# Twelve output stores issued from ScalarE's queue instead of SyncE's, in a windowed-attention and gated-MLP kernel

## The chip, the cores and the metric

The kernel runs on one core of one Trainium2 chip. A core has a matrix engine (TensorE, PE in the profile), three engines for elementwise work (VectorE, DVE; ScalarE, ACT; GpSimd, POOL), an engine that only issues transfers (SyncE, SP) and 16 DMA engines. Each of the five takes its instructions from a list of its own. ScalarE can issue a transfer too: the instruction that does so stands in its list between its arithmetic. An instruction that needs the result of another engine, or the end of a transfer, waits for a semaphore.

The metric is the device time of one execution in microseconds (us), as a median of several runs. Lower is better.

## The reference

Eight batches, eight heads of width 64, 512 local tokens and 32 global tokens for each batch. Global tokens attend to everything, local tokens to the 32 global ones and to the local ones at most 32 places away. The result of attention, 4608 tokens of 512 values, goes through a gated MLP. Cut to what matters:

```
k_all, v_all = concatenate([k_g, k_l]), concatenate([v_g, v_l])
out_g = softmax(q_g @ k_all.T / 8) @ v_all
s_l = concatenate([q_l @ k_g.T / 8, where(|i - j| <= 32, q_l @ k_l.T / 8, -1e9)])
out_l = softmax(s_l) @ v_all
x = concatenate([out_g, out_l]) as 4608 x 512
xn = x / sqrt(mean(x * x) + 1e-6) * rms_g
g, val = xn @ w_gate, xn @ w_val            # 512 -> 1536
out = (g * sigmoid(g) * val) @ w_out        # 1536 -> 512
```

## The kernel before, in words

**Chunks.** The tokens are worked off in nine chunks. Chunks 0 to 7 are the 512 local tokens of one batch each, chunk 8 holds the 256 global tokens of all batches. While the MLP of chunk c is on TensorE, the attention of a later chunk and the norm of chunk c + 1 are woven between its products. In chunks 0 and 1 the weights are also prepared. Weights and activations are split into two fp16 parts each, high and low, and every product is done in three passes (high by high, high by low, low by high).

**The products.** From chunk 2 on, the first layer of a local chunk is done as a 2 x 2 block product by seven products instead of eight (`moe_pair`, results in the banks `pq`). From chunk 3 on the second layer is done by seven products as well (`moe_out`, L1547 to 1640, results in the banks `pr`); chunk 8 has a plain first layer (`moe_f`, results `p`) and this second layer at half the width. Chunks 0 to 2 store their outputs by other code, which is not touched.

**Inside the second layer.** The seven products are numbered. Numbers 1, 5 and 6 are summed alongside each other, and then 2, 7, 3 and 4 are added onto the banks of 1, 6, 5 and 6. As a number ends, `rest(p)` evicts it: 1 gives a tile `os` (ScalarE), 6 gives `oq` (ScalarE, then GpSimd) and the second half of `os` (VectorE). The two output tiles `oo0` and `oo1` hold the two halves of the chunk's tokens: 2 gives one half of `oo0` (ScalarE), 7 one half of `oo1` (VectorE), 3 the other half of `oo0` (VectorE), and then `store(0)` is called, 4 the other half of `oo1` (VectorE), and then `store(1)`. A store of chunks 3 to 7 moves 256 x 512 float32 (512 KB) to the output, one of chunk 8 half of that. That makes twelve stores.

**The next chunk's operands.** Its activations `x` (for chunk 8 `xg`) become fp16: `xh` is the high part, a cast on ScalarE, `xl` the low part, a subtraction of the two on VectorE or GpSimd. The seven-product form also needs sums `h` of blocks, split into `ht` in the same way: a cast on ScalarE, a subtraction on VectorE. In attention, `e` are the exponentials (ScalarE), `sm` their sums, `et` the exponentials transposed (VectorE), and `a` the bank into which TensorE multiplies them by the values `v`.

**What sets the order.** Every call from chunk 1 on is first recorded with its engine by `write` (L1910), under a step's name, and then replayed in the order of hand-written tables, one for each chunk (`_ORDER_1` to `_ORDER_8`). So each engine's list follows the tables, and the profile gives all of these instructions the line of the recorder, L1929. A call that moves to another engine keeps its place in the table and stands in the other engine's list. The loads of weights come from SyncE as well: `fetch` (tiles `wt`, first layer) and `fetch_out` (tiles `wu`, second layer, from the arrays `wa` and `wb`), taken out of a ring when they are due.

**Buffers.** `wt`, `wu`, `os`, `oq`, `oo0`, `oo1` and several tiles of the first layer (`u`, `v`, and others) share one pool of twelve equal buffers (tag `wf`). A new tile takes a buffer whose last users have to be done: for a stored tile that is the end of its transfer.

Of the kernel before, what the change touches and what calls it, by code (L numbers as in the profile page):

```python
# [279 lines left out]
def attention_moe_kernel(  # L280
# [17 lines left out]
    nc = tc.nc  # L298
# [147 lines left out]
    def attn_bank(name):  # L446
        return psum.tile([P, 512], F32, tag="pa", bufs=4, name=name)
# [1099 lines left out]
    def moe_out(ch, c, n, row):  # L1547

        st, w, nj = {}, n // 2, n // 256
        onto = {2: 1, 7: 6, 3: 5, 4: 6}  # L1550

        def bank(p):
            if p not in onto and p not in st:
                if p == 5:
                    st[p] = (
                        attn_bank(f"pr{p}")
                        if c == B
                        else psum.tile([P, 512], F32, tag="pv", bufs=1, name=f"pr{p}")
                    )
                else:  # L1560
                    st[p] = psum.tile([P, 512], F32, tag="po", bufs=2, name=f"pr{p}")
                return st[p], True
            return st[onto.get(p, p)], False

        def products(i):
            for b in (2 * i, 2 * i + 1):
                doing(c, f"O{b}")
                p, g = BLOCKS[b]
                ps, first = bank(p)
                hi, lo = ch["hp"][p, g]  # L1570
                u = ch["wu", b]
                for j in range(nj):
                    for a, x in ((0, hi), (0, lo), (1, hi)):
                        nc.tensor.matmul(
                            ps[:, j * HT : (j + 1) * HT],
                            x[:, j * P : (j + 1) * P],
                            u[:, a, :],
                            start=first,
                            stop=(p in (2, 3, 4) and g == NF // 2 - 1 and a == 1),
                            skip_group_check=True,  # L1580
                        )
                        first = False

        def tile(name):
            t = pool.tile([P, 2, 512], F32, tag="wf", bufs=NF, name=f"{name}_{c}")
            return t

        def part(p):
            return st[onto.get(p, p)][:, : nj * HT]

        def flat(name, i):
            return st[name][:, i, : nj * HT]

        def result(z, h):
            if ("o", z) not in st:
                st["o", z] = tile(f"oo{z}")
            return st["o", z][:, :nj, h * HT : (h + 1) * HT]

        def put(z, h, p, x):
            o = result(z, h)  # L1600
            ps = part(p).rearrange("p (j n) -> p j n", j=nj)
            if x is None:
                nc.scalar.mul(o, ps, inv_k)
            else:
                nc.vector.scalar_tensor_tensor(
                    o, ps, inv_k, x.rearrange("p (j n) -> p j n", j=nj), ALU.mult, ALU.add
                )

        def store(z):
            to = out[row + z * w : row + (z + 1) * w, :].rearrange("(j p) d -> p j d", p=P)  # L1610
            nc.sync.dma_start(to, st["o", z][:, :nj, :])

        def rest(p):
            if p == 1:
                st["s"], st["q"] = tile("os"), tile("oq")
                nc.scalar.mul(flat("s", 0), part(1), inv_k)
            elif p == 6:
                nc.scalar.mul(flat("q", 0), part(6), inv_k)
                nc.vector.scalar_tensor_tensor(
                    flat("s", 1), part(5), inv_k, flat("s", 0), ALU.mult, ALU.add  # L1620
                )
                nc.gpsimd.tensor_tensor(flat("q", 0), flat("q", 0), flat("s", 0), ALU.add)
            elif p == 2:
                put(0, 0, 2, None)
            elif p == 7:
                put(1, 1, 7, flat("s", 1))
            elif p == 3:
                put(0, 1, 3, flat("q", 0))
                store(0)
            elif p == 4:  # L1630
                put(1, 0, 4, flat("s", 0))
                store(1)

        def after(i):
            ended = [p for p, g in BLOCKS[2 * i : 2 * i + 2] if g == NF // 2 - 1]
            if not ended:
                return None
            return lambda: [rest(p) for p in ended]

        return [(lambda i=i: products(i), after(i)) for i in range(len(BLOCKS) // 2)]  # L1640
# [182 lines left out]
    for c in range(NCH):  # L1823
# [3 lines left out]
        for i, un in enumerate(units):  # L1827
# [6 lines left out]
            for name, fn, pe, after in steps:  # L1834
                st = {"name": name, "unit": i, "fn": fn, "pe": pe, "c": c, "x": xi, "after": [], "at": None}
# [83 lines left out]
    def doing(c, step):  # L1919
        if at_work[:2] != [c, step]:  # L1920
            at_work[:] = c, step, 0, ""
# [14 lines left out]
    nc = Written  # L1936
# [231 lines left out]
```

## Time and profile before

| | |
|---|---|
| median of 3 runs | 904.91 us (904.52 to 905.95) |
| profiled execution, its own time | 906.6 us |
| its span, first to last instruction | 904.8 us |
| mean granted TensorE clock in it | 0.991 of full speed |
| TensorE busy | 867.7 us (96%) |
| VectorE busy | 725.8 us (80%) |
| ScalarE busy | 555.3 us (61%) |
| GpSimd busy | 277.2 us (31%) |
| moved by DMA | 212.03 MB, mean 234 GB/s |

How to read the lines that follow in the text: a row of the timeline gives the start of a group of like instructions in us from the start of the span, its length in us, the engine, the line, the operation, the tiles it writes and reads, the shape of one and the count; in brackets stand the idle time of the engine ahead of it and what ended that. Numbers of buffers and chunks are left out of the names, so `oo` is any of the output tiles. `SPq` and `ACTq` are the issues of transfers by SyncE and ScalarE. A row of the waits gives who waited for whom, then the total in us, the count and the longest. The trace puts a wait down to the one that came last.

### The profile page before, as it was taken

What the parts mean: (1) busy time and instruction counts of PE and PEld (TensorE: products, weight loads), DVE (VectorE), ACT (ScalarE), POOL (GpSimd) and SP (SyncE); (2) the same over time, 40 slices, a digit from 0 to 9 for tenths busy, and PEclk for the clock granted to TensorE, in tenths of its full rate; (3) what the DMA queues carried; (4) which work ended last, traced back from release to release, by engine and by line L of the source; (5) the groups of instructions that cost most, each with busy time, mean ns of one, the idle gap of its engine ahead of it and who ended that gap; (6) DMA issues with size and microseconds to landing.
All of it is one profiled execution on the core that took longest, in us unless ns stands there. A gap on an engine that the chain in (4) does not pass through costs nothing. (4 is left out here: it accounts for less than half of the span.)

```text
span 904.8 us, 27760 instructions
## 1 busy us (share of the span) xinstructions
PE 867.7 (96%) x11430; PEld 667.4 (74%) x11430; DVE 725.8 (80%) x1831; ACT 555.3 (61%) x1341; POOL 277.2 (31%) x244
## 2 busy tenths in 40 slices
PE   6699979999999998999999999999999999999998
PEld 4544445545547885588888888888888888888887
DVE  6899998988787687878987888789877886787554
ACT  6899997547354666357665856668565852456232
POOL 0000000033335676515521344223521453134311
PEclk9699999999999999999999999999999999999999
DMA  9983625499277786698778777777876666888675
GB/s 331 406 288 126 196 69 171 153 290 305 75 216 254 224 266 205 195 318 248 222 268 272 247 225 254 267 234 252 282 244 206 227 206 211 261 245 274 218 244 181
DMA packets 101007, 212.03 MB, mean 234 GB/s; under 512 B 8081, under 2 KB 34449, under 8 KB 100881
## 3 DMA queue, kind: packets, MB, share of 16 engines
q1 hardware_dynamic: 100448, 209.94, 70.7%
q8 instruction: 89, 1.46, 0.7%
q10 hardware_dynamic: 432, 0.33, 0.1%
q14 instruction: 38, 0.30, 0.1%
HBM read 183.24 MB, written 27.00 MB: 232 GB/s over the span
## 5 line engine op out<-in xcount | busy, mean ns | idle before, releaser
L1929 PEld LDWEIGHTS <-wt 128*128 128x128 f16 x3312 | 321.6, 98 | 46.3 <-issue 7.0
L1929 PE MATMUL pq<-xh,wt 128*128 128x256 f16 x1152 | 204.0, 273 | 1.3 <-DVE s L1929 1.3
L1929 PE MATMUL pq<-ht,wt 128*128 128x256 f16 x1296 | 156.4, 273 | 1.9 <-DVE v L1929 1.3
L1929 PE MATMUL pq<-xl,wt 128*128 128x256 f16 x576 | 157.0, 273 | 0.0
L1929 ACT ACTIVATE e<-e,sm 128x128 f32<-128x128 f32 x288 | 104.3, 390 | 8.4 <-DVE sm L1929 8.4
L1929 POOL TENSOR_TENSOR e<-e,sm 128x512 f32<-128x512 f32 x24 | 29.2, 1225 | 217.2 <-DVE sm L1929 211.0
L1929 PE MATMUL pr<-wu,hs 128*128 128x256 f16 x792 | 92.6, 273 | 1.2 <-DMA wu<-wb 1.2
L1929 POOL TENSOR_TENSOR hs<-u,hs 128x512 f16<-128x512 f32 x50 | 61.1, 1236 | 97.1 <-ACT hs L1929 92.1
L1929 POOL TENSOR_TENSOR hu<-v,hu 128x256 f16<-128x256 f32 (+1 forms) x60 | 57.1, 966 | 106.3 <-ACT hu L1929 93.0
L1929 PEld LDWEIGHTS <-hs 128*128 128x128 f16 x792 | 77.3, 98 | 10.7 <-issue 1.8
L1929 PE MATMUL pr<-wu,hu 128*128 128x256 f16 x594 | 70.2, 273 | 0.6 <-ACT os L1929 0.6
L1929 ACT ACTIVATE t<-u,half_inv 128x512 f32<-128x512 f32 x72 | 50.3, 718 | 30.9 <-DVE u L1929 29.2
L1929 DVE TENSOR_TENSOR v<-pq,s 128x512 f32<-128x512 f32 x72 | 49.3, 685 | 20.3 <-PE pq L1929 17.4
L1929 PEld LDWEIGHTS <-hu 128*128 128x128 f16 x594 | 57.9, 98 | 7.6 <-issue 0.9
L1929 PE MATMUL po<-wo,h 128*128 128x512 f16 x288 | 63.6, 379 | 0.0
L1651 PE MATMUL p<-xh,wf 128*128 128x512 f16 x192 | 58.8, 379 | 3.4 <-DVE t L1763 1.5
L1929 DVE TENSOR_TENSOR s<-pq,s 128x512 f32<-128x512 f32 x66 | 44.5, 684 | 20.2 <-ACT s L1929 11.2
L1929 ACT COPY s<-pq 128x512 f32<-128x512 f32 x72 | 41.4, 582 | 30.7 <-PE pq L1929 22.2
L1929 DVE SCALAR_TENSOR_TENSOR t<-t,u 128x512 f32<-128x512 f32 x72 | 54.8, 768 | 5.1 <-ACT t L1929 4.9
L1929 PE MATMUL p<-xh,wf 128*128 128x512 f16 x192 | 58.6, 379 | 0.0
L1651 PEld LDWEIGHTS <-wf 128*128 128x128 f16 x288 | 27.7, 98 | 38.2 <-issue 4.4
L1929 ACT COPY u<-pq 128x512 f32<-128x512 f32 x36 | 21.0, 583 | 51.7 <-PE pq L1929 50.9
(380 smaller groups left out, 1704.3 us busy)
## 6 DMA issues: line engine op xcount, KB each, us to landing
wt<-wd SPq DMA_DIRECT2D x120, 512.0 KB, 5.8
wu<-wb SPq DMA_DIRECT2D x36, 512.0 KB, 5.9
wr<-in_w_in_dram SPq DMA_DIRECT2D x24, 512.0 KB, 8.9
wu<-wa SPq DMA_DIRECT2D x24, 512.0 KB, 4.6
k<-in_qkb_dram SPq DMA_DIRECT2D x24, 448.0 KB, 7.1
gkq<-in_gkq_dram SPq DMA_DIRECT2D x16, 576.0 KB, 7.5
wt<-wd SPq DMA_DIRECT2D x36, 256.0 KB, 4.4
v<-in_vb_dram SPq DMA_DIRECT2D x24, 352.0 KB, 5.6
```

What stands on the lines that cost most here:

```text
L1651: nc.tensor.matmul(ps[:, :n], rows[:, a, o : o + P], ch[z][k][:, :n], start=(k == 0 and i == 0), stop=(k == NK - 1 and i == 2),)
L1929: return lambda *a, **k: write(self.engine, lambda: call(*a, **k))
```

## The change

In `store(z)` of `moe_out`, the transfer is issued by ScalarE instead of SyncE. Its place in the order of calls is the same, and so are its source, its target and its size.

```
         def store(z):
             to = out[row + z * w : row + (z + 1) * w, :].rearrange("(j p) d -> p j d", p=P)
-            nc.sync.dma_start(to, st["o", z][:, :nj, :])
+            nc.scalar.dma_start(to, st["o", z][:, :nj, :])
```

SyncE's list loses twelve instructions and ScalarE's gains them; the lists of VectorE, GpSimd and TensorE keep their order. In the rows below a name's numbers are its kind, its chunk or pair, and the buffer; `out_0_dram` is the output.

First, ScalarE's list in the second layer of chunk 4, around the eviction of product 1 (`os_4`) and product 6 (`oq_4`), with the semaphores that each waits for:

```order
@@ -528,6 +530,6 @@
 L1929 CAST hu5_2928<-v_5_2904 128x1024
 L1929 CAST hs5_2930<-u_5_2907 128x1024 [waits DVE_49]
-L1929 ACTIVATE os_4_2939<-pr1_2912,kk_91 128x512 [waits DMAHW0_49,PE_49,DMAHW3_49,Activation_49,Pool_49]
-L1929 ACTIVATE oq_4_2940<-pr6_2924,kk_91 128x512 [waits PE_49,Pool_49]
+L1929 ACTIVATE os_4_2939<-pr1_2912,kk_91 128x512 [waits DMAHW7_49,PE_49]
+L1929 ACTIVATE oq_4_2940<-pr6_2924,kk_91 128x512 [waits PE_49,DMAHW0_49,Activation_49,Pool_49]
 L1929 ACTIVATE e1201_2937,sm12_2914<-e1201_2937,sm12_2914 128x128 [waits DVE_49] x2
```

No instruction moved, but the shared pool hands `os_4` another buffer: it no longer waits for GpSimd (`Pool`), and `oq_4` waits as before for GpSimd and for a transfer besides.

Second, the same list some twenty rows later, at the store of `oo1` of chunk 4, among the exponentials `e1210` and `e1211` of a later chunk's attention:

```order
@@ -526,4 +528,5 @@
 L1929 CAST xh53_2953<-x5_2_2901 128x512
 L1929 ACTIVATE e1210_2931<-e1210_2931,sm12_2914 128x128 x4
+L1929 DMA out_0_dram<-oo1_4_2956 128x2x512
 L1929 ACTIVATE e1211_2945<-e1211_2945,sm12_2914 128x128 x4
 L1929 CAST xh55_2943<-x5_0_2773 128x512
```

The store now stands between the two groups of four, and the second group and the cast `xh55` stand behind it.

Third, ScalarE's list at the end of chunk 6, where `xh7` and `ht7` are operands of chunk 7:

```order
@@ -705,5 +711,7 @@
 L1929 CAST xh72_3314<-x7_2_3277 128x512
 L1929 ACTIVATE oo0_6_3316<-pr1_3288,kk_91 128x2x256
+L1929 DMA out_0_dram<-oo0_6_3316 128x2x512
 L1929 CAST xh73_3318<-x7_2_3277 128x512
+L1929 DMA out_0_dram<-oo1_6_3321 128x2x512
 L1929 CAST ht77_3311<-h7_4_3313 128x512
 L1929 COPY s6_0_3330<-pq6_0_3326 128x512
```

Both stores come in, and the cast `ht77` stands behind the second. At the end of chunk 3 it is alike: the store of `oo1_3` stands ahead of the cast `xh45`. In chunk 5 that of `oo1_5` stands ahead of ScalarE's half of `oo0_5`.

Fourth, ScalarE's list at the end of chunk 7, where `xh8` are operands of chunk 8 and `t` belong to its first layer:

```order
@@ -771,6 +779,8 @@
 L1929 CAST xh81_3476<-xg_77 128x256
 L1929 CAST xh82_3477<-xg_77 128x256
+L1929 DMA out_0_dram<-oo1_7_3483 128x2x512
 L1929 CAST xh83_3478<-xg_77 128x256
 L1929 ACTIVATE oo0_7_3471<-pr1_3449,kk_91 128x2x256
+L1929 DMA out_0_dram<-oo0_7_3471 128x2x512
 L1929 ACTIVATE t1_3493<-p0_1_3491,half_inv_79 128x256
 L1929 ACTIVATE t0_3487<-p0_0_3486,half_inv_79 128x256
```

The store of `oo1` stands ahead of the cast `xh83` and of ScalarE's half of `oo0`. In chunk 8 the two stores are the last instructions of ScalarE's list.

## The prediction

> **What bounds the kernel now.** I read the busy table first, then what TensorE (PE) waits for in the part of the run in which the changed stores stand, then the groups of the stored tiles, then the timeline around each store. The busy table:
>
> ```profile
> span 904.8 us, 27760 instructions
> ...
> PE 867.7 (96%) x11430; PEld 667.4 (74%) x11430; DVE 725.8 (80%) x1831; ACT 555.3 (61%) x1341; POOL 277.2 (31%) x244
> ```
>
> PE is the bound. The matmul waits from 460 us to the end, in which all twelve stores fall, have as columns the total, the count and the longest, in us:
>
> ```profile
> PE pq L1929 <- DVE v L1929: 1.3, 1, 1.3
> PE pq L1929 <- DVE s L1929: 1.3, 1, 1.3
> PE pr L1929 <- DMA wu<-wb: 1.2, 1, 1.2
> PE pr L1929 <- ACT os L1929: 0.6, 1, 0.6
> ```
>
> PE stands still there for 4.4 us in 445, and none of it is put down to a store. So moving stores can win at most a little, and what holds PE up anywhere is paid for in full. The stores themselves, as waits of SyncE (SP) and as a group:
>
> ```profile
> SPq L1929 <- DVE oo L1929: 43.9, 12, 7.5
> ...
> L1929 SPq DMA_DIRECT2D out_dram<-oo x12: 338/378/389, 475.5 to 901.9; - x12
> ```
>
> Each store waits on SP for VectorE's (DVE's) last half of its tile, 43.9 us over twelve, and takes 0.34 to 0.39 us to issue. ScalarE's (ACT's) issue is in the trace too, once beside SP's and once behind another of its own:
>
> ```profile
> 0.73 0.41 ACTq L326 DMA_DIRECT2D mask<-in_masks_dram  x1
> 0.74 0.39 SPq L665 DMA_DIRECT2D q<-in_qk_dram  x1
> 1.17 0.46 ACTq L328 DMA_DIRECT2D gcol<-in_rms_g_dram  x1
> ```
>
> I take 0.41 us for an issue on ACT and 0.04 us per hand-over. The second ACT issue starts 0.03 after the first ends; other hand-overs below show up to 0.08.
>
> **Part by part.** The bytes are the same, and the twelve issues leave SP. On ACT a store brings two prices: its issue, and its wait for DVE, during which ACT, which takes its instructions in their order, starts nothing that stands behind. Whether that reaches PE depends on those instructions. I go through the places in the order of the chunks.
>
> Chunk 3. The second store stands ahead of the cast xh45 that begins the last operands of a first-layer product:
>
> ```profile
> 477.34 0.61 ACT L1929 CAST xh<-x 128x512 f16<-128x512 f32 x1
> ...
> 478.88 0.75 DVE L1929 SCALAR_TENSOR_TENSOR oo<-pr,kk,os 128x512 f32<-128x512 f32 x1 [1.45 <-PE pr L1929]
> ...
> 479.55 0.71 DVE L1929 TENSOR_TENSOR xl<-x,xh 128x512 f16<-128x512 f32 x1
> ...
> 481.41 0.27 PE L1929 MATMUL pq<-xl,wt 128*128 128x256 f16 x1
> ```
>
> The tile is ready at 479.63 (478.88 + 0.75). Then 0.04, 0.41 of issue, 0.04, 0.61 of cast, 0.04, 0.71 of the subtraction and 0.04 give 481.52, against PE's 481.41: **+0.11**. Before, the cast was done ahead of time.
>
> Chunk 4, a gain. The pool of tiles hands os another buffer (the order below the diff shows its waits change), one that GpSimd (POOL) does not read:
>
> ```profile
> 553.30 1.47 PE L1929 MATMUL pr<-wu,hu 128*128 128x256 f16 x12
> ...
> 555.92 0.69 ACT L1929 ACTIVATE os<-pr,kk 128x512 f32<-128x512 f32 x1 [3.68 <-POOL hu L1929]
> ...
> 556.66 2.12 PE L1929 MATMUL pr<-wu,hu 128*128 128x256 f16 x18 [0.57 <-ACT os L1929]
> ```
>
> os then starts when PE has ended its sum, at 554.77, and is done by 555.5, over 1 us before PE wants the bank back: **−0.57**, the gap in brackets.
>
> Chunk 4, the loss. The second store stands between two groups of four exponentials; the later group is wanted by two transposes and then by PE:
>
> ```profile
> 570.05 1.26 ACT L1929 ACTIVATE e<-e,sm 128x128 f32<-128x128 f32 x4
> ...
> 571.37 0.70 DVE L1929 SCALAR_TENSOR_TENSOR oo<-pr,kk,os 128x512 f32<-128x512 f32 x1
> 572.00 1.28 DVE L1929 STREAM_TRANSPOSE et<-e 128x512 f32<-128x512 f32 x2
> ...
> 573.92 0.82 PE L1929 MATMUL a<-et,v 32*64 32x256 f32 x27
> ```
>
> Ready at 572.07; plus 0.04 + 0.41 + 0.04 + 1.26 + 0.04 + 1.28 + 0.04 is 575.18, against 573.92: **+1.26**. DVE takes the transpose of the later group first, so both count.
>
> Chunk 5. The second store stands ahead of ACT's half of the other tile:
>
> ```profile
> 669.75 0.75 DVE L1929 SCALAR_TENSOR_TENSOR oo<-pr,kk,os 128x512 f32<-128x512 f32 x1 [1.25 <-PE pr L1929]
> ...
> 672.14 0.37 ACT L1929 COPY x<-a 128x256 f32<-128x256 f32 x1 [3.29 <-PE a L1929]
> ...
> 675.89 1.47 PE L1929 MATMUL pq<-ht,wt 128*128 128x256 f16 x12
> ```
>
> ACT was idle for 3.29 us up to 672.14, so the issue (from 670.54) and that 0.7 us half (the same form's 0.69 below) end by 671.8, inside the idle time. PE uses the bank at 675.89: **0**. Without that cover it would be about 1.1.
>
> Chunk 6. The second store stands ahead of the cast ht77, and DVE's difference ht and subtraction xl follow that cast in one line:
>
> ```profile
> 763.02 0.62 ACT L1929 CAST ht<-h 128x512 f16<-128x512 f32 x1
> ...
> 766.02 0.74 DVE L1929 SCALAR_TENSOR_TENSOR oo<-pr,kk,os 128x512 f32<-128x512 f32 x1
> 766.68 0.68 DVE L1929 TENSOR_TENSOR ht<-h,ht 128x512 f16<-128x512 f32 x1
> 767.28 0.69 DVE L1929 TENSOR_TENSOR xl<-x,xh 128x512 f16<-128x512 f32 x1
> ...
> 768.48 0.27 PE L1929 MATMUL pq<-xl,wt 128*128 128x256 f16 x1
> ```
>
> Ready at 766.76; plus 0.04 + 0.41 + 0.04 + 0.62 + 0.04 + 1.29 (ht and xl, 766.68 to 767.97) + 0.04 is 769.24, against 768.48: **+0.76**. The cast xh73 stands between the two stores and now runs behind the first one's issue; if that pushes the second by an issue's length, it is 0.41 more.
>
> Chunk 7. The store of oo1 stands ahead of the cast xh83, POOL's subtraction follows that, and PE needs both for chunk 8:
>
> ```profile
> 851.47 0.40 ACT L1929 CAST xh<-xg 128x256 f16<-128x256 f32 x1 [2.13 <-DVE xg L1929]
> 851.95 0.67 POOL L1929 TENSOR_TENSOR xl<-xg,xh 128x256 f16<-128x256 f32 x1 [0.80 <-ACT xh L1929]
> 852.22 0.69 ACT L1929 ACTIVATE oo<-pr,kk 128x512 f32<-128x512 f32 x1 [0.35 <-PE pr L1929]
> ...
> 856.15 0.75 DVE L1929 SCALAR_TENSOR_TENSOR oo<-pr,kk,os 128x512 f32<-128x512 f32 x1 [4.38 <-PE pr L1929]
> ...
> 857.04 0.27 PE L1929 MATMUL p<-xl,wt 128*128 128x256 f16 x1
> ```
>
> Here the wait is longest: ACT cast at 851.47, and now stands still until 856.90. Then 0.04 + 0.41 + 0.04 + 0.40 + 0.08 (ACT's end at 851.87 to POOL's start) + 0.67 + 0.04 give 858.58, against 857.04: **+1.54**.
>
> The two last stores. DVE's last half is the end of the work:
>
> ```profile
> 901.35 0.48 DVE L1929 SCALAR_TENSOR_TENSOR oo<-pr,kk,os 128x256 f32<-128x256 f32 x1 [1.43 <-PE pr L1929]
> ```
>
> The last store leaves at 901.83 either way: 0.41 on ACT for at most 0.39 on SP, **0** (to within 0.1).
>
> SP gets its 43.9 us of waits back, so loads that stood behind stores go earlier. Only the 1.2 us wait for wu could gain: between nothing, as I take it, since that load waits for its buffer (rivals), and −1.2.
>
> The sum is 0.11 − 0.57 + 1.26 + 0.76 + 1.54 = **+3.10 us**, on the profiled run: span 904.8 to 907.9. That run lies 1.8 us above its span and 1.7 above the median of 904.91; the same addition there gives **908.0 us**. Hand-overs of 0 or of 0.08 in place of 0.04 move the four places by 0.5 each way, and chunk 6 can add 0.4: the forecast's own range is 907.4 to 909.0.
>
> The Trainium skill, page "DMA: Bandwidth & Descriptors", section "Issuing engines are not separate DMA queues", says that DMAs started from several engines run on the same DMA engines and that this saves only the sequencer's time to initiate. By that rule twelve issues of 0.378 us, 4.5 us of SP, are all that changes, and the kernel stays at 904.9. It doesn't count the wait that the sequencer takes along, which by the SP row is ten times as large.
>
> **Rivals.** *No change (0.15).* PE had gaps of its own after two of the places, 1.3 and 1.3 us at pq and 1.2 at wu, and a stall before a gap can come out of it. The wait for wu traces back to PE itself in the chain of waits:
>
> ```profile
> 732.87 0.59 ACT u L1929
> ...
> 746.27 2.11 POOL hu L1929 x2
> 748.38 6.85 DMA wu<-wb
> ```
>
> ACT's u here follows PE's own product, then POOL, then the load, so a PE that is late makes this wait late too; that speaks against. If instead the 1.3 and the 1.2 swallow chunk 4's term and ACT's casts are partly ahead, 906.2 to 906.7 is left. The Trainium skill's rule above, taken alone, would put it here at 904.9.
>
> *Faster (0.04).* If ACT did not hold later instructions while a store waits, the losses vanish, and os' 0.57 and the 1.2 of wu are won: 904.91 − 1.8 = 903.1, just at the bound of what counts as faster below. Against it: the wu load starts at 748.38, behind POOL and not behind a store, and ACT's idle brackets show it waiting in line.
>
> *Slower still (0.09).* An issue of SP next to DMA traffic can take far longer than 0.4:
>
> ```profile
> 767.26 2.25 SPq L1929 DMA_DIRECT2D wt<-wd  x1
> ```
>
> In chunks 3, 4 and 6 SP's next load now starts together with the store on ACT, as both wait for the same end on DVE. If one such issue on ACT is stretched like this (2.25 − 0.41 = 1.8), it gives 909.8; all of the four places, up to 915. Against it: at 0.73 and 0.74 both engines issued at once in 0.41 and 0.39. The point from which it decides is an ACT issue of over 1 us. The Trainium skill's "Perfetto Trace Analysis", section "DMA Instruction — HWDGE (DVE, Sync)", draws such a wait for a shared descriptor block; only the stretched SP row is in keeping with it.
>
> **How the numbers follow.** The forecast has 0.72. About 0.2%, 1.8 us, is what a measurement of this kernel can tell from no change, so the bounds are 903.1 and 906.7. Faster 0.04 and no change 0.15 are the rivals' own chances; the forecast (907.4 and up) and the worse case are slower: 0.81. The range reaches from 906.3, which takes in most of the no-change case that the stalls leave, to 909.8, one stretched issue.
>
> **What would show it.** In the changed trace: PE gaps of about 1.3 before a<-et,v at 574, 0.8 before pq<-xl at 769 and 1.5 before p<-xh or p<-xl at 857, put down to ACT, DVE or POOL; ACT standing still behind DVE oo, 5 us of it in chunk 7; no gap for os near 556; no waits on DVE oo left on SP. I am wrong if PE has no new gaps there, if ACT's store issue is long, or if the gap at 755 goes with the stores.

## The result, and the profile after

| | before | after |
|---|---|---|
| median of four executions each, same comparison | 905.23 us (904.52 to 905.95) | 913.38 us (911.04 to 913.60) |
| ratio, 95% interval | 1 | 1.0073 (1.0056 to 1.0090) |
| profiled execution, its own time | 906.6 us | 913.29 us |
| its span | 904.8 us | 911.2 us |
| mean granted TensorE clock in it | 0.991 | 0.987 |

The kernel is slower, by more than twice the 3.1 us forecast: 0.73% of 905 us is 6.6 us, between 5.1 and 8.1 by the interval. (The ratio is not the quotient of the two medians, which lie 8.15 us apart; this text goes by the ratio.) The side was right, the size and the range were not.

The first lines of the page of after: the same instructions, 6.4 us more span, and TensorE longer at work, which with the same matmuls means a slower clock in places.

```profile
span 911.2 us, 27760 instructions
...
PE 871.4 (96%) x11430; PEld 667.7 (73%) x11430; DVE 727.9 (80%) x1831; ACT 555.6 (61%) x1341; POOL 277.4 (30%) x244
```

What TensorE waited for from 384 us on in after (who, for whom, total, count, longest):

```profile
PE pq L1929 <- DVE xl L1929: 2.0, 1, 2.0
PE pq L1929 <- DVE v L1929: 1.3, 1, 1.3
PE pq L1929 <- DVE s L1929: 1.3, 1, 1.3
PE pr L1929 <- DMA wu<-wa: 0.8, 2, 0.5
PE p L1929 <- ACT xh L1929: 0.7, 1, 0.7
PE a L1929 <- DVE et L1929: 0.7, 1, 0.7
PE p L1929 <- POOL xl L1929: 0.5, 1, 0.5
```

The waits for v and s are those of before. New are the one for xl (chunk 6), for et (chunk 4), and for xh and xl ahead of p (chunk 7): the three places of the prediction. The wait for os is gone. The waits for loads have changed places; more on them below. What ScalarE waited for, and the stores as a group:

```profile
ACT xh L1929 <- DVE oo L1929: 14.7, 3, 8.0
...
L1929 ACTq DMA_DIRECT2D out_dram<-oo x12: 351/378/436, 475.8 to 908.2; - x12
...
DMA to landing us min/median/max: 2.0/5.8/7.0
```

The casts xh waited 14.7 us in three places for a stored tile that they do not read: that is the hold in the queue. The issues themselves are short, 0.35 to 0.44 us, and none is stretched.

**Where the time went, place by place.** I took the start of the same matmul in two traces and the change of the difference from one side of a place to the other (480 to 486 us of before for chunk 3, 554 to 560 for os, 572 to 576 for chunk 4, 758 to 769 for chunk 6, 769 to 771 for what follows it, 856 to 860 for chunk 7). This leaves out what differs elsewhere. In us, with three profiles of the changed kernel (the second and third are runs below):

| place | forecast | after | second | third |
|---|---|---|---|---|
| chunk 3 | +0.11 | +0.51 | +0.50 | +0.50 |
| os of chunk 4 | −0.57 | −0.73 | −0.73 | −0.73 |
| chunk 4 | +1.26 | +1.18 | +1.02 | +1.02 |
| chunk 6 | +0.76 | +2.38 | +2.45 | +2.26 |
| behind chunk 6 | – | +1.42 | +1.35 | +1.54 |
| chunk 7 | +1.54 | +1.52 | +1.51 | +1.51 |
| sum | +3.10 | +6.28 | +6.10 | +6.10 |

From 460 us to the end, where all the stores lie, TensorE loses 6.14, 5.43 and 5.52 us against before in the three profiles. So the places hold the change, and the rest, −0.1 to −0.7 us, is what differs elsewhere, the waits for loads among it. The +1.18 of chunk 4 holds a small gap further on in the product a as well: in the four kernels that leave chunk 4's stores and the order as they were, this window differs from before by −0.13 to +0.45 us.

Chunk 6 and what follows it take 3.80 us in each profile, 3.04 more than forecast. Nearly all that was missed lies there. Its rows in after, ScalarE first, then GpSimd, VectorE and TensorE:

```profile
766.80 0.38 ACTq L1929 DMA_DIRECT2D out_dram<-oo  x1
767.22 0.62 ACT L1929 CAST xh<-x 128x512 f16<-128x512 f32 x1 [4.00 <-DVE oo L1929]
767.40 0.38 ACTq L1929 DMA_DIRECT2D out_dram<-oo  x1
767.82 0.62 ACT L1929 CAST ht<-h 128x512 f16<-128x512 f32 x1
...
767.92 1.16 POOL L1929 TENSOR_TENSOR xl<-x,xh 128x512 f16<-128x512 f32 x1 [8.23 <-ACT xh L1929]
769.03 1.60 POOL L1929 TENSOR_TENSOR ht<-h,ht 128x512 f16<-128x512 f32 x1
...
768.48 1.15 DVE L1929 TENSOR_TENSOR ht<-h,ht 128x512 f16<-128x512 f32 x1 [1.10 <-ACT ht L1929]
769.54 1.64 DVE L1929 TENSOR_TENSOR xl<-x,xh 128x512 f16<-128x512 f32 x1
...
771.23 0.27 PE L1929 MATMUL pq<-xl,wt 128*128 128x256 f16 x1 [1.98 <-DVE xl L1929]
```

In before, GpSimd had the same two operations at another time:

```profile
763.20 1.16 POOL L1929 TENSOR_TENSOR xl<-x,xh 128x512 f16<-128x512 f32 x1 [5.39 <-ACT xh L1929]
764.31 1.16 POOL L1929 TENSOR_TENSOR ht<-h,ht 128x512 f16<-128x512 f32 x1
```

The first store holds the cast xh73, and so GpSimd's pair moves from 763 to 768 (all of TensorE's work is 0.6 us later there) and lies beside VectorE's pair. There VectorE takes 1.15 and 1.64 us for what took 0.68 and 0.69, and GpSimd 1.60 for 1.16. The starts and ends read like turns: VectorE's xl starts at 769.54, GpSimd's ht ends at 770.63, and VectorE ends 0.55 after that. The Trainium skill, page "SBUF — State Buffer", section "SBUF: two separate sides", says that VectorE with two SBUF inputs and GpSimd share a pair of ports as an exclusive lock. By that rule the pairs go one after the other, and the trace agrees, with 1.64 = 1.09 of waiting + 0.55.

Behind the gap TensorE is slow for a while. The windows of after, with TensorE's busy time first and the granted clock as the third number from the end:

```profile
769.00:771.00 2.00, 0.25 (x3) 0.08 (x1) 2.00 (x2) 0.58 (x1) 1.63 (x2) 1.00 0.94 329
771.00:773.00 2.00, 1.77 (x10) 1.31 (x10) 0.78 (x2) 0.58 (x1) 0.00 (x0) 0.63 0.90 348
773.00:775.00 2.00, 2.00 (x12) 1.37 (x11) 0.69 (x1) 0.00 (x0) 0.00 (x0) 0.52 0.53 143
775.00:777.00 2.00, 2.00 (x20) 1.79 (x19) 0.08 (x1) 0.00 (x0) 0.00 (x0) 1.00 0.89 290
```

The clock falls to half after the 1.98 us gap and is back at 775: about 3.4 us at half speed. This costs 1.66 us in each of the three profiles: the 1.4 of the table, and some slow matmuls that lie ahead of the table's border at 769. Up to the matmul that waits, chunk 6 costs 2.14 us.

### The profile page after: what moved, and what is told of

Same layout as the page of the kernel before. It is cut to its first block, busy times and chain, and to the rows that moved or that the text cites. A ratio compares the mean times of both kernels' runs of the same rounds, so it can differ in the third digit from the quotient of the medians.

```text
span 911.2 us, 27760 instructions
## 1 busy us (share of the span) xinstructions
PE 871.4 (96%) x11430; PEld 667.7 (73%) x11430; DVE 727.9 (80%) x1831; ACT 555.6 (61%) x1341; POOL 277.4 (30%) x244
## 5 line engine op out<-in xcount | busy, mean ns | idle before, releaser
L1929 PEld LDWEIGHTS <-hs 128*128 128x128 f16 x792 | 77.2, 98 | 10.2 <-issue 1.1
```

What stands on the lines that cost most here:

```text
L1929: return lambda *a, **k: write(self.engine, lambda: call(*a, **k))
```

## The experiments

Theory H is that of the prediction, with chunk 6 read anew: ScalarE holds everything behind a store until VectorE has ended the tile. Theory Q, the rival: the transfers themselves cost, since on a second queue, beside SyncE's loads, they land late (5.8 us median, 3.8 before) and keep loads and buffers waiting. Where a kernel has some stores on ScalarE and the rest on SyncE, its edit is the line

```
-            nc.sync.dma_start(to, st["o", z][:, :nj, :])
+            (nc.scalar if (c, z) in STORES else nc.sync).dma_start(to, st["o", z][:, :nj, :])
```

with the STORES named below. Ratios are to the kernel before in the same comparison, with 29 or 35 executions of it and 12 of each kernel (6 in each of the two unchanged repeats of after).

**The first store of chunk 6 alone**, STORES = (6, 0).

> Only the first store of chunk 6 (oo0) goes to ScalarE, the other eleven stay on SyncE. Theory H (ScalarE holds what stands behind a store): xh73 is cast after the store, so GpSimd's xl and ht start near 767.5 instead of 763 and run beside VectorE's ht and xl, which then take about 1.1 and 1.6 us instead of 0.68 and 0.69; a PE gap of 1.5 to 2 us ahead of pq<-xl, and a stretch at half clock behind it (another 1.5) where the gap is long enough: 2 to 3.5 us over the kernel before. Theory Q (the stores' transfers on a second queue hold up loads): under 0.3 us, since one store of twelve moved, and no gap at pq<-xl.

1.0011 (0.9994 to 1.0028), at most 2.5 us. In the trace chunk 6 costs 2.17 us and no other place more than 0.13. VectorE and GpSimd:

```profile
766.86 1.23 DVE L1929 TENSOR_TENSOR ht<-h,ht 128x512 f16<-128x512 f32 x1 [1.05 <-ACT ht L1929]
768.01 1.64 DVE L1929 TENSOR_TENSOR xl<-x,xh 128x512 f16<-128x512 f32 x1
...
766.39 1.15 POOL L1929 TENSOR_TENSOR xl<-x,xh 128x512 f16<-128x512 f32 x1 [9.77 <-ACT xh L1929]
767.50 1.60 POOL L1929 TENSOR_TENSOR ht<-h,ht 128x512 f16<-128x512 f32 x1
```

The same overlap as in after, from one store, and a gap of 2.01 us. The clock did not fall behind it here: the next matmuls keep their pace. The last section shows why.

**The second store of chunk 6 alone**, STORES = (6, 1).

> Only the second store of chunk 6 (oo1) goes to ScalarE. Theory H: xh73 is cast early as in the kernel before, GpSimd's xl and ht are done before VectorE's, which keep 0.68 and 0.69 us; only the cast ht77 is late: a PE gap of 0.7 to 0.8 us ahead of pq<-xl, full clock behind it, +0.8 us over the kernel before. If the issue on ScalarE itself were the cost, this and the run with the first store alone would cost the same. Theory Q: under 0.3 us.

1.0016 (1.0001 to 1.0032). Chunk 6 costs 0.75 us in the trace: the 0.76 of the prediction, to a hundredth. VectorE and GpSimd:

```profile
769.65 0.69 DVE L1929 TENSOR_TENSOR ht<-h,ht 128x512 f16<-128x512 f32 x1 [1.13 <-ACT ht L1929]
770.26 0.69 DVE L1929 TENSOR_TENSOR xl<-x,xh 128x512 f16<-128x512 f32 x1
...
764.96 1.15 POOL L1929 TENSOR_TENSOR xl<-x,xh 128x512 f16<-128x512 f32 x1 [4.00 <-ACT xh L1929]
766.07 1.15 POOL L1929 TENSOR_TENSOR ht<-h,ht 128x512 f16<-128x512 f32 x1
```

GpSimd is done before VectorE starts, and both have their old durations. So it is the first store, which the prediction passed over, that makes the dear part.

**All stores on ScalarE, moved to the end of each chunk's order** (chunk 7: only the store of oo1 moved, to the last place):

```
 _ORDER_6 (and likewise 3, 4, 5)
-... R59.0 R59.1 n54.1 n55.0 O41.0 R62.0 R62.1 n55.1 n56.0 n53.1 n52.0
+... R59.0 n54.1 n55.0 O41.0 R62.0 n55.1 n56.0 n53.1 n52.0 R59.1 R62.1
```

> All twelve stores on ScalarE, but in chunks 3 to 7 moved to the end of the chunk's order, behind the casts and exponentials that the next chunk waits for. Theory H: no PE gaps near 574, 769 and 857, full clock there; what is left is the eviction os of chunk 4 without its wait (-0.6) and small waits for loads either way: within 1.5 us of the kernel before, 903.5 to 906.5. Theory Q: the transfers are the same as in the changed kernel and land as late, so most of its 8 us stays: 910 to 913.

1.0025 (1.0005 to 1.0044), 2.3 us: much less than the changed kernel, and yet more than the 1.5 us that theory H allowed. The gaps near 574 and 769 are gone. The expected gain at os did not come, as that tile kept its old buffer. Two other gaps are there, in TensorE's waits:

```profile
PE pq L1929 <- DVE u L1929: 1.4, 1, 1.4
...
PE p L1929 <- DVE t L1929: 0.9, 1, 0.9
```

The second is the hold again: two issues stand at 859.45 ahead of chunk 8's first eviction t. The first is theory Q's: VectorE's v waits there for a semaphore of a transfer and starts when a store of chunk 3 has landed, whose buffer v takes:

```profile
491.41 0.69 DVE L1929 TENSOR_TENSOR v<-pq,s 128x512 f32<-128x512 f32 x1 [4.04 <-PE pq L1929]
492.02 0.68 DVE L1929 TENSOR_TENSOR u<-pq,s 128x512 f32<-128x512 f32 x1
```

The bracket names pq, but in before v starts at 486.61, directly behind s, so its product was done long before. That store was issued at 482.23 and landed at 491.29. So a late store can cost through its buffer, but it does so where it is issued late, not in the changed kernel, where no TensorE gap traces to it.

**The wait without the transfer.** All stores on SyncE; in `store` ScalarE copies two columns that span both halves of the tile to a scratch tile first (the order tables get the extra step behind each store's):

```
+            nc.scalar.copy(seen_o, st["o", z][:, 0, HT - 1 : HT + 1])
             nc.sync.dma_start(to, st["o", z][:, :nj, :])
```

> All stores stay on SyncE; at each store's place ScalarE copies two columns of the stored tile (one from each half) to a scratch tile that nobody reads, so that it waits for VectorE as the store would, without any transfer. The outputs are unchanged. Theory H: the same PE gaps as in the changed kernel, near 574, 769 and 857, each shorter or longer by the difference between this copy (0.2 to 0.3 us) and the store's issue: +5 to +7 us. Theory Q: within 0.5 us of the kernel before.

1.0037 (1.0020 to 1.0054). The copies are short, and ScalarE stands still for VectorE ahead of them:

```profile
L1929 ACT COPY seen<-oo x12: 177/193/194, 479.4 to 908.8; 128x2 f32<-128x2 f32 x12
...
DVE oo L1929: 27.1, 8
```

The places cost +0.22 (chunk 3), +0.76, +1.82 and +1.19 (chunks 4, 6, 7), 4.0 together, with the same releasers on TensorE:

```profile
PE pq L1929 <- DVE xl L1929: 1.7, 1, 1.7
...
PE p L1929 <- POOL xl L1929: 0.5, 1, 0.5
PE p L1929 <- ACT xh L1929: 0.4, 1, 0.4
...
PE a L1929 <- DVE et L1929: 0.3, 1, 0.3
```

That is less than the 5 to 7 expected: by about 0.3 us at each of the four places (in chunk 6 counted up to the matmul that waits), and by the fall of the clock, which does not come behind the 1.66 us gap. The 0.3 is the issue itself: in chunk 7 the cast xh starts 0.10 us after the start of the copy, at 862.60, and in after 0.42 after the start of the store, at 861.78. No transfer moved, and most of the price is there. Wait (4.0), issue (4 x 0.3), clock (1.66) and os (−0.73) add up to the 6.1 of the changed kernel, so nothing is left there for theory Q.

**The changed kernel again**, no edit, for more executions.

> The changed kernel once more, in many executions beside the kernel before on one chip, since single executions of the kernel before spread there from 904.4 to 911.2 us. Theory H with the terms measured so far (chunk 4 +1.2, chunk 6 +2.0 to 2.4, chunk 7 +1.2 to 1.5, os of chunk 4 -0.6, 1.5 to 1.7 more in executions whose TensorE clock drops behind the gap of chunk 6): +4 to +6 us over the kernel before. If the first comparison (+8.15 of four executions each) holds, 3 us more are still to be found: theory Q or another place. PE gaps near 574, 769 and 857 as before; waits for loads near 421, 645, 755 and 828 change from profile to profile.

1.0078 (1.0048 to 1.0108); medians 911.66 and 906.83. The places are the column "second" above.

**All but chunk 6**, STORES = all but (6, 0) and (6, 1).

> Ten stores on ScalarE, the two of chunk 6 on SyncE. Theory H: the run above less chunk 6: no gap ahead of pq<-xl near 769, GpSimd's and VectorE's subtractions apart again, no clock drop there; 2 to 4 us faster than all twelve on ScalarE, +1.5 to +3 over the kernel before. Theory Q: 2 of 12 of the changed kernel's cost less, about 1 us.

1.0031 (1.0017 to 1.0046), 2.8 us where the places sum to 2.3. Chunk 6 costs 0.01 us and the clock stays. Two stores of twelve carry more than half of the price.

**Chunk 4 alone**, STORES = (4, 0), (4, 1).

> Only the two stores of chunk 4 on ScalarE. Theory H: a gap ahead of a<-et,v near 574 that moves PE by 1.2 to 1.3 us; os of chunk 4 keeps its GpSimd wait (0.57), since the buffers ahead of it are as before; +1.2 us over the kernel before. Theory Q: 0.2 to 0.7, and no PE gap at a<-et,v.

1.0026 (1.0006 to 1.0047). The place costs 1.05 us, and os keeps its wait, as expected; the time, 2.4 us by the ratio, is above that, but its interval (0.5 to 4.3) takes it in:

```profile
PE a L1929 <- DVE et L1929: 0.7, 1, 0.7
PE pr L1929 <- ACT os L1929: 0.6, 1, 0.6
```

TensorE starts the product with two matmuls on time and then waits 0.7 us; by the end of the product, 576 us, it is 1.05 late.

**Chunk 7 alone**, STORES = (7, 0), (7, 1).

> Only the two stores of chunk 7 on ScalarE. Theory H: two gaps near 857, one ahead of p<-xh and one ahead of p<-xl, 1.2 to 1.5 us together, ScalarE's cast xh held until VectorE's last half of oo1; +1.3 us over the kernel before. Theory Q: 0.2 to 0.7, and no PE gap.

1.0031 (1.0015 to 1.0047). The place costs 1.54 us, the forecast's figure; the time, 2.8 us by the ratio (1.4 to 4.3), takes it in.

**The changed kernel a third time**, as the measure for the next run.

> The changed kernel, as the measure for the next one, which differs from it in the place of one cast. From the terms measured: c3 +0.4, os -0.7, chunk 4 +1.3, chunk 6 +2.1 and 1.5 for the clock behind it, chunk 7 +1.5, together +6.1 us over the kernel before, between 4.5 and 8 by what the first two comparisons gave.

1.0074 (1.0047 to 1.0101); medians 913.83 and 906.74. Column "third" above.

**The changed kernel with one cast moved**: in chunk 6 the first store goes behind the cast xh73.

```
 _ORDER_6
-... R59.0 R59.1 n54.1 n55.0 O41.0 R62.0 R62.1 ...
+... R59.0 n54.1 n55.0 R59.1 O41.0 R62.0 R62.1 ...
```

> All twelve stores on ScalarE, and in chunk 6 the cast xh73 goes ahead of the first store instead of behind it; nothing else moves. If GpSimd's late subtractions beside VectorE's make the second and larger half of chunk 6's price, they now start about 4 us earlier, VectorE's ht and xl fall from 1.15 and 1.64 to 0.69 and 0.69, the gap ahead of pq<-xl falls from 2.0 to 0.6-0.8 us and the clock does not drop behind it: 2.5 to 3 us faster than the run above. If VectorE's long operations have another cause (the stores' transfers), they stay long and nothing is won.

1.0040 (1.0022 to 1.0057): 3.1 us faster than the run above by the two ratios, 4.0 by the medians (909.87 for 913.83). Chunk 6 costs 0.73 us for 2.26, and nothing behind it for 1.54, together 3.07 less. VectorE and GpSimd:

```profile
770.37 0.69 DVE L1929 TENSOR_TENSOR ht<-h,ht 128x512 f16<-128x512 f32 x1 [1.10 <-ACT ht L1929]
770.98 0.68 DVE L1929 TENSOR_TENSOR xl<-x,xh 128x512 f16<-128x512 f32 x1
...
765.70 1.15 POOL L1929 TENSOR_TENSOR xl<-x,xh 128x512 f16<-128x512 f32 x1 [4.01 <-ACT xh L1929]
766.81 1.16 POOL L1929 TENSOR_TENSOR ht<-h,ht 128x512 f16<-128x512 f32 x1
```

Both stores are still on ScalarE, and only GpSimd's work came out from beside VectorE's. With this the cause of chunk 6 is shown: not the issue, not the transfer, but whom the held cast feeds.

**All stores on ScalarE, each directly behind what the next chunk waits for** (`_ORDER_3`: R62.1 behind n53.1; 4: R62.1 behind n55.0; 6: R59.1 and R62.1 at the end; 7: R62.1 behind R59.0).

> All twelve stores on ScalarE, each directly behind the last instruction that the next chunk waits for: chunk 3 behind xh45 and ht47, chunk 4 behind the second group of exponentials, chunk 6 behind ht77, chunk 7 behind xh83 and ScalarE's half of oo0. Theory H: no gaps near 481, 574 and 769, a gap of up to 0.5 us near 858, where the two issues stand ahead of chunk 8's first eviction; os -0.6. Within 1 us of the kernel before. If stores on ScalarE's queue land late and hold buffers (as in the run with the stores at the chunks' ends, where VectorE waited 1.4 us for a stored buffer), a gap near 490 stays and it is 1 to 2 us slower than before.

1.0020 (1.0005 to 1.0035), 1.8 us where 1 was expected. No gap is left near 481 and 769, 0.34 near 862, as expected. The os gap stayed, against the expectation, and there was a 2.2 us gap within the attention product a, ended by "issue"; the other profiles have 0 to 0.5 us at that matmul, with chunk 4's stores on ScalarE or not. What makes it is open.

**Chunks 3 and 5 alone**, STORES = (3, 0), (3, 1), (5, 0), (5, 1).

> Only the four stores of chunks 3 and 5 on ScalarE. Theory H: os of chunk 4 gets the other buffer and its 0.57 us gap near 556 goes; chunk 3's late cast xh45 costs 0.1 to 0.45 near 481 to 484; chunk 5 nothing. -0.6 to +0.2 us: not to be told from the kernel before by the times, only by the trace.

0.9995 (0.9977 to 1.0012): no difference to be told. In the trace os gains 0.73 and chunk 3 costs 0.50, so the other buffer for os comes from the stores of chunk 3. No version tried is shown to be faster than the kernel before.

## Why the prediction was right in its side and wrong in its size

**The mechanism** was right: TensorE is the bound, the stores' bytes do not matter, and a store that waits in ScalarE's list holds what stands behind it. The wait without a transfer gives most of the price by itself.

**Chunk 4 and chunk 7** were right: 1.26 forecast, 1.02 to 1.18 measured (1.02 at the wait itself in all three profiles), and 1.54 forecast, 1.51 measured. Chunk 7 shows every step of that chain: the store at 861.78 for 0.38, then

```profile
862.20 0.41 ACT L1929 CAST xh<-xg 128x256 f16<-128x256 f32 x1 [8.02 <-DVE oo L1929]
...
862.65 0.27 PE L1929 MATMUL p<-xh,wt 128*128 128x256 f16 x1 [0.71 <-ACT xh L1929]
863.40 0.27 PE L1929 MATMUL p<-xl,wt 128*128 128x256 f16 x1 [0.48 <-POOL xl L1929]
```

The hand-overs are 0.04 here too. **os** was right in kind, −0.73 for −0.57: the bracket counts from the end of the last matmul, which is 0.27 us long, while in a run of matmuls the next starts 0.11 after it. So a gap in brackets is 0.16 short of the delay, here as in chunk 6 (1.98 and 2.14). **Chunk 5 and the last stores** cost nothing, as forecast.

**Chunk 6 is the step that failed**: forecast 0.76, with 0.41 more as the worst that the first store could do. That followed only ScalarE's own list: the cast xh73 would be late, and with it the second store. It didn't follow whom xh73 feeds. GpSimd's two subtractions stood on nobody's path in before, so the working left them out; started 4.7 us later (763.20 to 767.92, 0.6 of it the delay of the whole kernel), they lie beside VectorE's, and VectorE is on the path. This brought 1.4 us (2.14 up to the matmul that waits, for 0.76), and behind the gap, now 2 us long instead of 0.6, the clock fell, another 1.66 that the sum did not have at all. Both together are the 3 us that were missed. The fall is in part luck of the execution (see the last section): without it the places sum to 4.5 us, still above the 2.5 to 4.1 of the forecast's own range.

**Chunk 3** was forecast at 0.11 for xl, and at that matmul PE is late by 0.09. Another 0.42 follows at 484 us, in the global attention's product gs. In the run with chunks 3 and 5 alone it waits 0.3 us for a copy x of VectorE and 0.2 for a copy s of ScalarE. VectorE's copy is late for the reason found in chunk 6. The cast behind xh45 is held too, GpSimd's pair starts at 481.54 in after for 478.55 in before, and beside it VectorE's ht takes 1.65 us for 0.68:

```profile
482.65 1.61 POOL L1929 TENSOR_TENSOR xl<-x,xh 128x512 f16<-128x512 f32 x1
...
483.17 1.65 DVE L1929 TENSOR_TENSOR ht<-h,ht 128x512 f16<-128x512 f32 x1
```

So the same step of the working failed here a second time, in small.

**The rivals.** No change did not come: the waits of TensorE behind the places did not swallow the stalls. The wait of 1.2 us for wu in before, which the prediction weighed, is gone at 755 in all three profiles of the changed kernel, and the prediction had named that as a sign of being wrong. But it is no fixed thing: at the same matmul it is 1.47 and 0 us in the two kernels with one store of chunk 6 moved, where nothing ahead of it had changed. Nor does the load leave earlier: it is issued at 748.38 in before and at 750.26 in after, where TensorE is 1.9 us late; only its landing differs. SP's relief does not show there. The stretched issue did not come either, at most 0.44 us on ScalarE. By the rule of the Trainium skill, page "DMA: Bandwidth & Descriptors", section "Issuing engines are not separate DMA queues", only the time to initiate would have moved; the trace does not agree, since the sequencer's wait moved too, and with what followed from it the change cost 6 us.

**What stays open**: the 2.2 us in one profile, and why the same load lands sooner in one execution than in another. The interval of the measured change, 4.3 to 9.8 us over the three comparisons, holds the 6.1 to 6.3 of the places, but cannot confirm them to better than that.

## What to carry to other kernels

A transfer put into the list of an engine that computes brings its wait along: ask not what the issue costs but what stands behind it, and follow each held instruction to everyone that it feeds, engines with time to spare included, since work that may be late can still land beside work that may not. A store belongs behind the last instruction of its list that somebody waits for, or in a list in which nothing else is urgent. A gap of about 2 us has a price beyond its length in those executions in which the clock falls behind it.

## What the runs showed of the hardware

**The clock falls behind gaps of about 2 us, sometimes.** In fourteen profiles, from 340 us on, ten TensorE gaps of 1.9 to 2.2 us occur. Behind six of them the clock is at half for about 3.4 us, 1.7 us of time lost; behind four it is not. Behind gaps of up to 1.75 us it never is, unless a longer one follows. One of the falls, seen from the gap's end to 3.4 us on, in the third profile of the changed kernel, and then the gap and the stretch behind it in the run with the first store of chunk 6 alone, where the clock stays at 1.00:

```profile
768.40:771.80 3.40, 3.40 (x18) 2.44 (x18) 1.24 (x2) 0.59 (x1) 0.00 (x0) 0.56 0.74 224
771.80:775.00 3.20, 3.20 (x30) 2.76 (x28) 0.69 (x1) 0.00 (x0) 0.00 (x0) 0.93 0.79 282
...
765.60:769.00 3.40, 2.09 (x20) 1.73 (x18) 2.35 (x3) 1.73 (x3) 2.61 (x2) 1.00 0.86 295
769.00:772.40 3.40, 2.70 (x25) 2.43 (x25) 1.94 (x3) 0.59 (x1) 0.10 (x1) 1.00 0.87 223
```

What decides is where the gap lies. In each profile all changes of the granted clock lie on a grid with steps of 3.413 us, and the grid lies elsewhere in each execution. The six gaps with a fall lie whole within one step, which so has 1.90 to 2.18 us of idle time, and the clock falls at the end of that step, for one step: in after the gap is 769.25 to 771.23, the step 768.11 to 771.52. The four without a fall are cut by a line of the grid, with at most 1.45 us on either side: in the run with the first store alone 1.34 and 0.67. Steps with up to 1.66 us have no fall. So from 340 us on the border lies between 1.66 and 1.90 us of idle time in one step. Near 120 us, where TensorE has other work, the clock falls behind steps with 1.3 us as well, so idle time alone is not the whole measure. An estimate from these numbers: a gap of 1.98 us falls whole into a step of 3.413 us in about four executions of ten (1.43 of 3.413), if the grid lies at random.

The Trainium skill, page "TensorE: Matmul & The Clock Gate", section "What's actually happening", has the clock fall after an idle window of about 3.4 us. Here 1.98 us of waiting within one step were enough, and what agrees is the length of the step and of the slow stretch.

**Executions of the same kernel spread.** The kernel before took 904.4 to 911.2 us in 35 executions on one chip. The fourteen profiles differ by up to 3.8 us by 300 us, before any of the stores of this study: by 1.8 at 45 us, where the clock's half-speed stretches differ (mean clock 0.77 to 0.89 there), and by 3.5 at 130 us, behind a half-speed stretch near 120 us that lasts 3.4 us in eleven of them, 10.2 in two and is missing in one. The 0.2% that the prediction took for what can be told was too fine for a handful of executions.
